# Second layer in pieces of 512, 512, 384, 384 and 384 columns, and a lag of three steps with loads two steps ahead in the first layer

## The chip, the cores and the metric

The kernel runs on one core of one Trainium2 chip. The metric is device microseconds of one execution. TensorE is PE in the rows (PEld its weight loads), VectorE is DVE, ScalarE is ACT, and SyncE is SP, whose queue issues nearly all DMAs.

## The reference, cut to what matters

```python
x, state: (8 batches, 8 heads, 512 | 32, 64)
a     = softmax(scale * x @ state.T);   xread = a @ state
a2    = softmax(scale * state @ x.T);   sread = a2 @ x
x = concat([xread, sread])              # 8 * (512 + 32) = 4352 tokens of 512
h = x @ w_in;  r = max(h, 0);  x = (s * r * r + b) @ w_out      # first layer, 512 -> 2048 -> 512
h = x @ w_in;  g = h / (1 + exp(-h));  out = g @ w_out          # second layer, same sizes
```

All is asked for in float32. The weights arrive as 64-bit floats.

## The kernel before, in words

**Precision.** Each factor of a product is split into a high and a low part (line 218 `copy` on ACT rounds to the high part, line 221 `rest` on DVE subtracts), and each product is three matmuls: high by high, high by low, low by high (lines 533 and 866).

**First layer.** Tokens are worked off in nine blocks (line 102): the 512 `x` tokens of each batch, blocks 0 to 7, and at last the 256 `state` tokens of all batches, block "s". Block 0 is interleaved by a list written out by hand (lines 36 to 77, `first`, line 1151) with the weight conversion and the attention of batches 0 and 1. The others go through `run` (line 627): a block has 16 steps, one for each 128 rows of the hidden layer. One step of a 512-wide block:

- `mm1_a` (line 538): six matmuls into a bank `ph` (pool of two banks);
- `act_a` (line 570): relu on ACT (572), `s*r*r` on DVE (573). The second half, `gh = r + b` on ACT (578) and `gl = r + b - gh` on DVE (579), is put off by `late` and issued by `finish` (line 559) at the beginning of the next step;
- `flush(LAG)` (line 655): `mm2_a` (line 597), twelve matmuls of 512 columns, for the step LAG = 2 before. When that was the last step of a block, `end_a` (line 611) follows: four banks are copied out (lines 606 and 608) and four DMAs write them to `x2` (line 618);
- the step's extras, `do(f, 0)` ahead of `mm1_a` and `do(f, 2)` at the end (line 1377 `extra`): the attention of the next batch, loads and splits of `G` (lines 308 and 318), and what `convert` (line 1262) has set down.

`r`, `gh` and `gl` have three buffers each (line 564).

**Conversion of the second layer's weights** runs beside blocks 1 to 7. `convert` gives each pair of weights six steps: `load64` (line 152, two DMAs of 512 KB into one of two `raw` buffers) ahead of step `at`, where `at` is 16 + 3u with u even; `absw` (line 176, ACT) at the end of step `at + 1`; then the bit operations (`bits`, line 180, DVE, four for each half of the pair), `reorder`, `keep` (a DMA to `kept`) and `sum_w` (four DVE operations and two DMAs). Block 2 begins with step 32, block 5 with step 80, so a pair's `load64` falls on step f = 2 of each of those two blocks.

In the rows ACT, DVE and SP each work through their instructions in program order.

**Block "s" and the places.** `last_block` (line 1286) hands tiles that are free by then to a queue `spare`; everything in the second layer takes its tiles from its front and gives them back at its end (`Place`, line 684). `v24` to `v31` are handed over at the first step, `wh` and `wl` of step f - 2 at step f (line 1304).

**Second layer.** Seven products in the place of eight (`PRODUCTS`, line 82, with sums of inputs and of weights). The tokens are cut into two halves of 2176, and each half into five pieces (lines 673 to 675): four of 448 columns and one of 384. `first_product` (line 967) goes through all pieces: for each, eight `Quad`s of seven steps with six matmuls each (line 867), 336 matmuls a piece. ACT copies and applies silu, DVE adds and subtracts, and the results go to DRAM (`go`, line 903), one DMA a step on the average. While a piece runs, the next one's inputs are loaded and split: 14 `high`s on ACT and 14 `low`s on DVE, one of each in a step, from step 46 of the piece's 56 (lines 1356 to 1358). The last A22 product of a Quad is put into step 2 of the next one (line 973).

Then `Chunks` (line 1080) does the second product in the same pieces: 56 chunks a piece, each with one load from `go` (line 1096), one high, one low and six matmuls, 336 a piece again. Loads run twelve chunks ahead. Every third step `load_o` (line 1446) loads output weights until all are there. Twelve chunk loads and the first twelve output weights are issued in the last piece of the first product (lines 1359 to 1367). Transposed results go out by `put` (line 1049).

Of the kernel before, what the change touches and what calls it, by code (L numbers as in the profile page):

```python
# [13 lines left out]
F32R = mybir.dt.float32r  # L14
# [10 lines left out]
NF = DFF // P  # L25
# [1 line left out]
NT = B * SB  # L27
SCALE = 0.125
EPS = 1e-9
LAG = 2  # L30
NU = 16
RING = 8

# [54 lines left out]
def fused_kernel(ctx: ExitStack, tc, xt, xn, sbd, sg, w1, w2, sv, bv, out):  # L88
# [32 lines left out]
    def space(tag, shape=(P, S), dtype=F32R):  # L121
        return wpool.tile(list(shape), dtype, tag=tag, name=tag)
# [3 lines left out]
    def rot(name, n, shape=(P, S), dtype=F32):  # L126

        i = turns[name] = turns.get(name, -1) + 1
        return space(f"{name}{i % n}", shape, dtype)
# [429 lines left out]
    def finish():  # L559

        while late:
            late.pop(0)()

    def new_act(n):
        r = rot("r", 3)
        gh = rot("gh", 3, dtype=F32R)
        gl = rot("gl", 3, dtype=F32R)
        return r[:, :n], gh[:, :n], gl[:, :n]

    def act_a(ph, n, bi):  # L570
        r, gh, gl = new_act(n)
        nc.scalar.activation(out=r, in_=ph[:, :n], func=AF.Relu)  # L572
        nc.vector.scalar_tensor_tensor(  # L573
            out=r, in0=r, scalar=s_sb, in1=r, op0=ALU.mult, op1=ALU.mult
        )

        def second():
            nc.scalar.activation(out=gh, in_=r, func=AF.Identity, bias=b_sb)  # L578
            nc.vector.scalar_tensor_tensor(  # L579
                out=gl, in0=r, scalar=b_sb, in1=gh.bitcast(F32), op0=ALU.add, op1=ALU.subtract  # L580
            )

        late.append(second)
        return gh, gl
# [12 lines left out]
    def mm2_a(f, g, n):  # L597
        gh, gl = g
        w = "o", f
        cs = [slice(c * P, (c + 1) * P) for c in range(NC)]  # L600
        mm2(f, [(wh[w][:, c], wl[w][:, c], gh[:, :n], gl[:, :n]) for c in cs], n)
# [9 lines left out]
    def end_a(k):  # L611
        n = width[k]
        for c in range(NC):
            o = pull_out(c, n)
            o = o[:, :n]
            if k == "s":
                o = o.rearrange("p (b r) -> p b r", r=NS)
            nc.sync.dma_start(out=rows(c, k), in_=o)
# [8 lines left out]
    def run(blocks, pend):  # L627


        def flush(upto):  # L630
            while len(pend) > upto:
                i, f, g = pend.pop(0)
                k = blocks[i]
                mm2_a(f, g, width[k])
                if f == NF - 1:
                    end_a(k)

        for i, k in enumerate(blocks):
            if i == 0:
                continue  # L640
            ops = extra(i)

            def do(f, when):
                for op in ops.get((f, when), ()):
                    op()

            for f in range(NF):
                do(f, 0)
                finish()
                pend.append((i, f, act_a(mm1_a(f, k), width[k], i)))  # L650
                do(f, 1)
                last = f == NF - 1 and i + 1 == len(blocks)
                if last:
                    finish()
                flush(LAG)
                if f == NF - 1 and not last:
                    prepare_a(blocks[i + 1])
                if last:
                    flush(0)
                do(f, 2)  # L660
# [10 lines left out]


    HALF = NT // 2
    WIDE = 448
    pieces = [(at, min(WIDE, HALF - at)) for at in range(0, HALF, WIDE)]
    sums = {(t, i, n): dram.tile([P, S], F32, name=f"sums_{t}{i}_{n}")
            for t in "IO" for i in range(NF // 2) for n in range(2)}
    go = {(k, p): dram.tile([NF // 2, P, n], F32, name=f"go_{k}_{p}")
# [3 lines left out]
    spare, fixed, closing = deque(), deque(), []  # L682
# [37 lines left out]
    def sub_(out, a, b):  # L720
        tt(out, a, b, ALU.subtract)
# [83 lines left out]
    class Inputs:  # L805
# [19 lines left out]
        def sum(self, name, c):  # L825
            to, a, b = {
                "T1": ("T1", "B12", "B11"), "T2": ("T2", "B22", "T1"),
                "T3": ("B12", "B22", "B12"), "T4": ("B21", "B21", "T2"),
            }[name]
            if (to, c) not in self.x:  # L830
                self.x[to, c] = Place(F32)
            to, a, b = (self.x[x, c] for x in (to, a, b))
            sub_(to.t[:, :self.n], a.t[:, :self.n], b.t[:, :self.n])
            self.x[name, c] = to
# [316 lines left out]
    def first():  # L1151

        halves = {n + str(b): Half(b, j) for b in range(2) for j, n in enumerate("pq")}
        act = {}
# [100 lines left out]

        for name in FIRST.split():
            one(name.rstrip("*"), name.endswith("*"))
        return [(0, f, act[f][1:]) for f in range(NF - LAG, NF)]

    later, quads = {}, {}  # L1260

    def convert():

        def add(at, when, op, *args):
            later.setdefault((at, when), []).append(lambda: op(*args))

        for u in range(2 * NF):
            i, t = u // 4, "IO"[u // 2 % 2]  # L1270
            pair = (t, i), (t, i + NF // 2)
            at = NF + 3 * u
            if u % 2 == 0:
                add(at, 0, load64, pair)
                add(at + 1, 2, absw, pair)
            for op, n in enumerate((2, 2, 3, 3)):
                add(at + n, 2, bits, pair, op, u % 2)
            if t == "O":
                add(at + 4, 2, reorder, pair, u % 2)
            add(at + 5, 2, keep, pair[u % 2])  # L1280
            if u % 2:
                x = sum_w(t, i)
                for n in range(5, 8):
                    add(at + n, 2, next, x)

    def last_block(add):

        def give(*tags):  # L1290
            add(f, 2, spare.extend, tags)

        splits = [(p, c) for p in RIGHT for c in range(2)]
        inputs[0] = Inputs(0)
        for f in range(NF):
            if f == 0:
                give("xt0", "xt1", "xn0", "xn1", *(f"mid{i}" for i in range(4)), "sbd",
                     "xh2", "xh3", "xl2", "xl3", *(f"v{i}" for i in range(24, 32)),
                     *(f"xr{i}" for i in range(4)))
                for i in range(2):  # L1300
                    add(f, 2, carve, f"raw{i}", 4)
                add(f, 2, inputs[0].load)
            if f >= 2:
                give(f"wh{f - 2}", f"wl{f - 2}")
            if f == 7:
                give(*(f"v{i}" for i in range(8, 16)))
            if f == 11:
                give(*(f"v{i}" for i in range(8)))
            if f == 15:
                give(*(f"v{i}" for i in range(16, 24)))  # L1310
            if 2 <= f < 4:
                for name in ("T1", "T2", "T3"):
                    add(f, 2, inputs[0].sum, name, f - 2)
            for i, what in ((f - 4, inputs[0].high), (f - 5, inputs[0].low)):
                if 0 <= i < len(splits) // 2:
                    for p, c in splits[2 * i:2 * i + 2]:
                        add(f, 2, what, p, c)
            for i, what in ((f - 6, "load"), (f - 9, "high"), (f - 10, "low")):
                if i >= 0 and i % 2 == 0 and i // 2 < 5:
                    if what == "load":  # L1320
                        quads[i // 2] = list(duos_in(i // 2))
                    for x in quads[i // 2]:
                        add(f, 2, getattr(x, what))
# [103 lines left out]
    with tc.manual_schedule():  # L1427

        warm = small.tile([P, 1], F32, tag="nm", name="warm")
        nc.gpsimd.memset(warm, 0.0)  # L1430
        nc.scalar.activation(out=warm, in_=warm, func=AF.Exp)
        make_identity(nc, ident)
        pend = first()
        convert()
        run(order, pend)
        spare.extend(f"{n}{i}" for n in ("wh", "wl") for i in (NF - 2, NF - 1))
        spare.extend(f"{n}{i}" for n in ("r", "o", "gh", "gl") for i in range(3))
        spare.extend(f"{n}{i}" for n in ("xh", "xl") for i in range(2))
        for tag in ("wf0", "wf1", "xs"):
            carve(tag, 2)  # L1440
        chunks = Chunks()
        to_load = iter([
            Duo(("O", i, p), ("O", i + 1, p)) for p in RIGHT for i in range(0, NF // 2, 2)
        ])

        def load_o(k=0, n=0):
            if k == 0 and n % 3 == 0:
                for x in islice(to_load, 1):
                    x.load()
                    after(6, x.high)  # L1450
                    after(7, x.low)

        steps = hooks(chunks, load_o)
        first_product(steps, lambda: chunks.step(load_o))
        while chunks.step(load_o):
            tick()
        while due:
            tick()
# [44 lines left out]
```

## Time and profile before

| what | us |
|---|---|
| median of 3 runs | 1374.11 |
| the runs | 1370.12, 1374.11, 1382.07 |
| the profiled execution | 1378.16 |
| its span in the trace | 1376.3 |
| PE busy in it | 1350.4 |

The rows below are from the profiled execution and count from the beginning of its span. A matmul's own duration in them is longer than the distance to the next one's start, since matmuls are pipelined; the distance of the starts is what a matmul costs. In rows of a timeline, idle time before the instruction stands in brackets with what ended it.

### The profile page before, as it was taken

Reading aid. Unit: us, or ns where it says so; the run is one execution under the profiler, and the core shown is the slowest. Engines: PE = TensorE matmul, PEld = TensorE weight load, DVE = VectorE, ACT = ScalarE, POOL = GpSimd, SP = SyncE. Lnnn points to the kernel's source line nnn. Section 1 sums busy time; section 2 is a strip of 40 time slices with the busy share of each in tenths; the row PEclk is TensorE's granted clock in tenths of the full one; section 3 lists DMA queues with packets and bytes.
Section 4 is the critical chain, followed back from the end, with each engine's and each line's share of the span. In section 5 each row is a group of like instructions: output and inputs, shape, how many; then the busy total and the mean of one; then the engine's idle time right before and its main releaser. Section 6 shows DMA issues by size and latency. Waiting matters only on the chain.

```text
span 1376.3 us, 19962 instructions
## 1 busy us (share of the span) xinstructions
PE 1350.4 (98%) x6648; PEld 1189.0 (86%) x6648; DVE 988.4 (72%) x1770; ACT 750.0 (54%) x1389; POOL 0.7 (0%) x7
## 2 busy tenths in 40 slices
PE   6999999999999999999999999999999999999998
PEld 4778888788888788888999999999998999999997
DVE  7899877788788778755877757575767756464655
ACT  7999644455545455444665646464656735353542
POOL 0000000000000000000000000000000000000000
PEclk9999999999999999999999999999999999999999
DMA  9999335454434535322648565656679895959593
GB/s 324 331 332 317 132 116 167 130 186 145 160 127 130 185 102 170 121 100 62 227 151 283 186 238 184 238 184 230 216 256 327 301 280 151 280 152 281 142 272 88
DMA packets 180999, 275.55 MB, mean 200 GB/s; under 512 B 22688, under 2 KB 133280, under 8 KB 180896
## 3 DMA queue, kind: packets, MB, share of 16 engines
q1 hardware_dynamic: 180096, 273.88, 60.6%
q8 instruction: 52, 0.85, 0.3%
q10 hardware_dynamic: 800, 0.39, 0.1%
q14 instruction: 51, 0.42, 0.1%
HBM read 158.34 MB, written 115.87 MB: 199 GB/s over the span
## 4 chain that ended last, share of the span: by engine, by line
PE 88%; DMA 4%; DVE 3%; ACT 2%; issue 1%; SPq 1%; DVEq 0%; ACTq 0%
PE bank L867 48%; PE o L593 24%; PE ph L534 12%; DMA raw<-w 3%; PE bank L509 2%; PE bank L270 2%; PE bank L534 1%; ACT xr L218 1%; DVE v L221 0%; PE bank L465 0%; DVE wf L195 0%; DMA go<-v 0%; ACT wf L178 0%; DMA xt<-xt 0%; DMA wl<-sums_O 0%
## 5 line engine op out<-in xcount | busy, mean ns | idle before, releaser
L593 PE MATMUL o<-gl,wh 128*128 128x512 f32 (+1 forms) x576 | 218.4, 379 | 3.7 <-DVE gl L579 3.6
L593 PE MATMUL o<-gh,wh 128*128 128x512 f32 (+1 forms) x576 | 218.4, 379 | 0.2 <-ACT gh L578 0.2
L593 PE MATMUL o<-gh,wl 128*128 128x512 f32 (+1 forms) x576 | 218.2, 379 | 0.0
L534 PE MATMUL ph<-xh,v 128*128 128x512 f32 (+1 forms) x640 | 204.9, 371 | 0.0
L572 ACT ACTIVATE r<-ph 128x512 f32<-128x512 f32 (+1 forms) x128 | 72.5, 566 | 145.5 <-PE ph L534 143.1
L573 DVE SCALAR_TENSOR_TENSOR r<-r,s_sb 128x512 f32<-128x512 f32 (+1 forms) x128 | 91.5, 715 | 68.5 <-ACT r L572 68.2
L534 PEld LDWEIGHTS ph<-xh,v 128*128 128x128 f32 x640 | 117.2, 189 | 20.2 <-ACT xr L218 0.5
L593 PEld LDWEIGHTS o<-gl,wh 128*128 128x128 f32 x576 | 108.8, 189 | 25.6 <-DVE gl L579 5.4
L593 PEld LDWEIGHTS o<-gh,wh 128*128 128x128 f32 x576 | 108.8, 189 | 20.6 <-ACT gh L578 0.6
L593 PEld LDWEIGHTS o<-gh,wl 128*128 128x128 f32 x576 | 108.7, 189 | 20.2
L579 DVE SCALAR_TENSOR_TENSOR gl<-r,b_sb,gh 128x512 fp32r<-128x512 f32 (+1 forms) x128 | 91.3, 713 | 42.3 <-ACT gh L578 41.6
L534 PE MATMUL ph<-xl,v 128*128 128x512 f32 (+1 forms) x320 | 117.8, 368 | 0.0
L578 ACT ACTIVATE gh<-r,b_sb 128x512 fp32r<-128x512 f32 (+1 forms) x128 | 88.6, 692 | 53.0 <-DVE r L573 53.0
L867 PE MATMUL bank<-v,v 128*128 128x448 f32 (+1 forms) x292 | 91.7, 360 | 0.0
L534 PEld LDWEIGHTS ph<-xl,v 128*128 128x128 f32 x320 | 60.4, 189 | 9.6
L218 ACT ACTIVATE v<-v 128x512 fp32r<-128x512 f32 (+2 forms) x103 | 60.6, 597 | 11.0 <-PE bank L867 6.9
L715 DVE TENSOR_TENSOR v<-bank,v 128x448 f32<-128x448 f32 (+1 forms) x49 | 29.7, 606 | 47.3 <-PE bank L867 43.9
L867 PEld LDWEIGHTS bank<-v,v 128*128 128x128 f32 x292 | 54.6, 188 | 3.9
L867 PE MATMUL bank<-v,wh 128*128 128x448 f32 (+1 forms) x163 | 54.1, 362 | 0.0
L867 PE MATMUL bank<-v,wl 128*128 128x448 f32 (+1 forms) x163 | 53.5, 361 | 0.0
L218 ACT ACTIVATE v<-bank 128x448 f32<-128x448 f32 (+1 forms) x42 | 22.3, 530 | 55.0 <-PE bank L867 54.5
L221 DVE TENSOR_TENSOR v<-v,v 128x512 fp32r<-128x512 f32 (+2 forms) x77 | 50.6, 665 | 1.5 <-ACT v L218 1.4
(1006 smaller groups left out, 3119.0 us busy)
## 6 DMA issues: line engine op xcount, KB each, us to landing
raw<-w SPq DMA_DIRECT2D x64, 512.0 KB, 6.0
v<-go SPq DMA_DIRECT2D x84, 224.0 KB, 4.3
go<-v SPq DMA_DIRECT2D x58, 224.0 KB, 2.3
gd<-xr SPq DMA_DIRECT2D x48, 256.0 KB, 4.0
go<-wl SPq DMA_DIRECT2D x44, 224.0 KB, 2.2
wl<-go SPq DMA_DIRECT2D x42, 224.0 KB, 4.5
v<-gd SPq DMA_DIRECT2D x32, 256.0 KB, 4.3
wh<-go SPq DMA_DIRECT2D x35, 224.0 KB, 4.2
```

Source lines behind the costliest of these rows:

```text
L218: nc.scalar.activation(out=out, in_=x, func=AF.Copy)
L221: nc.vector.tensor_tensor(out=lo, in0=x, in1=hi.bitcast(F32), op=ALU.subtract)
L270: nc.tensor.matmul(t, a[p][:, cs], x[w], start=i == 0, stop=i == 2)
L509: nc.tensor.matmul(o[:, k, :], xn_t[self.b, self.j, t // 2][:, t % 2, k * P:(k + 1) * P], self.a2[:, t * P + 2 * k * NS:t * P + 2 * (k + 1 ...
L534: nc.tensor.matmul(ph[:, :n], a, x, start=j == 0 and i == 0, stop=j == last and i == 2)
L572: nc.scalar.activation(out=r, in_=ph[:, :n], func=AF.Relu)
L573: nc.vector.scalar_tensor_tensor(out=r, in0=r, scalar=s_sb, in1=r, op0=ALU.mult, op1=ALU.mult)
L578: nc.scalar.activation(out=gh, in_=r, func=AF.Identity, bias=b_sb)
L579: nc.vector.scalar_tensor_tensor(out=gl, in0=r, scalar=b_sb, in1=gh.bitcast(F32), op0=ALU.add, op1=ALU.subtract)
L593: nc.tensor.matmul(po[c][:, :n], a, x, start=f == 0 and i == 0, stop=f == NF - 1 and i == 2)
L715: nc.vector.tensor_tensor(out=out, in0=a, in1=b, op=op)
L867: nc.tensor.matmul(bank[:, :n], a, x, start=start and j == 0 and i == 0, stop=stop and j == last and i == 2, skip_group_check=True,)
```

## The change

The second layer's pieces become 512, 512, 384, 384 and 384 columns (the sum is 2176 as before). In the first layer the lag goes from two steps to three; `gh` and `gl` get a fourth pair of buffers, `v30` and `v31`, from block 1 on, so that these two join `spare` only after `run`. In `convert`, all but the load of a pair comes one step later.

```diff
-LAG = 2
+LAG = 3
...
+    act_places = deque((f"gh{i}", f"gl{i}") for i in range(3))
+
     def new_act(n):
         r = rot("r", 3)
-        gh = rot("gh", 3, dtype=F32R)
-        gl = rot("gl", 3, dtype=F32R)
+        gh, gl = (space(tag) for tag in act_places[0])
+        act_places.rotate(-1)
         return r[:, :n], gh[:, :n], gl[:, :n]
...
-    WIDE = 448
-    pieces = [(at, min(WIDE, HALF - at)) for at in range(0, HALF, WIDE)]
+    widths = 512, 512, 384, 384, 384
+    pieces = [(sum(widths[:k]), n) for k, n in enumerate(widths)]
...
-        return [(0, f, act[f][1:]) for f in range(NF - LAG, NF)]
+        return [(0, f, act[f][1:]) for f in range(NF - 2, NF)]
...
-            at = NF + 3 * u
+            at = NF + 1 + 3 * u
             if u % 2 == 0:
-                add(at, 0, load64, pair)
+                add(at - 1, 0, load64, pair)
                 add(at + 1, 2, absw, pair)
...
-                     "xh2", "xh3", "xl2", "xl3", *(f"v{i}" for i in range(24, 32)),
+                     "xh2", "xh3", "xl2", "xl3", *(f"v{i}" for i in range(24, 30)),
...
         convert()
+        act_places.appendleft(("v30", "v31"))
         run(order, pend)
         spare.extend(f"{n}{i}" for n in ("wh", "wl") for i in (NF - 2, NF - 1))
         spare.extend(f"{n}{i}" for n in ("r", "o", "gh", "gl") for i in range(3))
+        spare.extend(("v30", "v31"))
```

## Rows read from the trace of the kernel before

**Rows 1.** The page, busy time of the engines (share of the span).
```profile
PE 1350.4 (98%) x6648; PEld 1189.0 (86%) x6648; DVE 988.4 (72%) x1770; ACT 750.0 (54%) x1389; POOL 0.7 (0%) x7
```

**Rows 2.** Waits of PE: us in total, times, longest.
```profile
PE o L593 <- DVE gl L579: 3.6, 3, 2.1
...
PE bank L867 <- DVE gl L221: 0.6, 1, 0.6
PE bank L867 <- DVE o L221: 0.4, 1, 0.4
```

**Rows 3.** Timeline of PE in the second layer: start, duration, instruction.
```profile
700.68 0.57 PE L867 MATMUL bank<-raw,wh 128*128 128x448 f32 x2
...
977.14 0.34 PE L867 MATMUL bank<-wl,wh 128*128 128x384 f32 x1
...
1035.59 0.37 PE L867 MATMUL bank<-xr,xn 128*128 128x448 f32 x1
...
1311.07 0.34 PE L867 MATMUL bank<-v,xn 128*128 128x384 f32 x1
...
1344.70 0.33 PE L867 MATMUL bank<-v,wl 128*128 128x384 f32 x1
...
1354.58 0.33 PE L867 MATMUL bank<-wl,wh 128*128 128x384 f32 x1
```

**Rows 4.** Chain that ended last, first layer: start, duration, what.
```profile
175.54 1.73 PE bank L509 x16
...
253.52 1.73 PE bank L509 x16
...
302.56 2.72 PE o L593 x12
...
398.81 1.73 PE bank L509 x16
...
472.98 1.73 PE bank L509 x16
...
545.64 1.73 PE bank L509 x16
```

**Rows 5.** Timeline of SP, beginning of block 2.
```profile
222.80 1.48 SPq L618 DMA_DIRECT2D x<-o  x3
...
226.22 1.28 SPq L157 DMA_DIRECT2D raw<-w  x2
```

**Rows 6.** Timeline of ACT, blocks 2 and 5.
```profile
235.20 1.12 ACT L178 ACTIVATE wf<-raw 128x1024 f32<-128x1024 f32 x1 [2.91 <-DMA raw<-w]
...
456.25 1.12 ACT L178 ACTIVATE wf<-raw 128x1024 f32<-128x1024 f32 x1 [0.70 <-DMA raw<-w]
```

**Rows 7.** Timeline of PE, block 2.
```profile
249.14 0.54 PE L593 MATMUL o<-gl,wh 128*128 128x512 f32 x1 [2.09 <-DVE gl L579]
...
250.33 0.63 PE L593 MATMUL o<-gl,wh 128*128 128x512 f32 x1
```

**Rows 8.** Windows: us, length, busy by engine (PE, PEld, DVE, ACT, POOL), granted clock, DMA share, GB/s.
```profile
250.00:252.00 2.00, 2.00 (x6) 1.56 (x5) 2.00 (x4) 1.50 (x3) 0.00 (x0) 0.50 0.02 7
...
460.00:464.00 4.00, 4.00 (x21) 3.30 (x20) 3.93 (x9) 1.28 (x3) 0.00 (x0) 1.00 0.00 0
...
1040.00:1060.00 20.00, 19.44 (x97) 17.67 (x96) 14.09 (x26) 11.98 (x24) 0.00 (x0) 1.00 0.99 336
```

**Rows 9.** Timeline of DVE, splits of the fourth piece's inputs, and 384-wide operations later.
```profile
898.58 0.62 DVE L221 TENSOR_TENSOR v<-xh,wl 128x448 fp32r<-128x448 f32 x1
...
908.88 0.62 DVE L715 TENSOR_TENSOR wh<-bank,wh 128x448 f32<-128x448 f32 x1
...
914.77 0.62 DVE L221 TENSOR_TENSOR wh<-r,xt 128x448 fp32r<-128x448 f32 x1
...
1039.64 0.55 DVE L715 TENSOR_TENSOR wl<-v,wl 128x384 f32<-128x384 f32 x1
1040.11 0.55 DVE L715 TENSOR_TENSOR v<-v,wh 128x384 f32<-128x384 f32 x1
```

## The prediction

> **What bounds the kernel now.** First the page: PE is busy 1350.4 of 1376.3 us [rows 1], so all idle time of PE together is 25.9 us, and a gain beyond some of that must come from matmuls that get cheaper. Then the waits of PE: 3.6 us behind `gl` in the first layer, 0.6 and 0.4 us in the second [rows 2]; the rest of the idle time lies at the two ends of the span, which the diff does not touch. A busy share does not say what one matmul costs, so next the timeline of PE, and in it the distances of the starts. In the first layer twelve matmuls of 512 columns take 2.72 us [rows 4], 226.7 ns each. In the second layer, 384-wide ones take (1354.58 - 1344.70) / 57 = 173.3 ns [rows 3] (57 matmuls lie between these two starts). At 2.4 GHz that is 544 and 416 cycles, columns plus 32 in both. The 448-wide ones should then take 200.0 ns. They don't: four pieces of 336, less the six that slip behind the next piece, take 977.14 - 700.68 = 276.46 us, which is 206.6 ns each, and PE waits for nothing there. In the second product, 1035.59 to 1311.07 holds 1344 of them, six of 384 (1.04 us) and the waits of 1.0 us [rows 2, 3]: 273.4 us, 203.5 ns each. So 448 columns are dear in this kernel, by 6.6 and 3.5 ns; why, no row says.
>
> Last the chain, which runs through PE nearly everywhere, and in it a mark that returns once in each block [rows 4]: 253.52 to 398.81 is two blocks, 72.65 us each; 472.98 to 545.64 is 72.66. But 175.54 to 253.52 takes 77.98 us, 5.33 too many, and 398.81 to 472.98 takes 74.17, 1.52 too many. Those are blocks 2 and 5. There ACT stood 2.91 and 0.70 us before `absw`, until the `raw` DMA had landed [rows 6]. SP had issued it at 226.22, behind the four writes of `end_a` from 222.80 on [rows 5]. Everything behind `absw` on ACT came late, relu and `gh` with it; DVE was full afterwards (3.93 of 4 us in 460 to 464) [rows 8] and `gl` came 2.09 us late for PE [rows 7]. After that wait the granted clock fell to 0.50, the 1.2 GHz level, in 250 to 252 [rows 8], where six matmuls stand in 2 us [rows 7, 8] in place of nine. So 6.85 us of the profiled execution are lost in two places of the first layer.
>
> **The widths.** The number of matmuls is the same (336 a piece in each product), the last piece is still 384 wide, and only the first four change. First product: 672 at 226.7 ns and 666 at 173.3 are 152.3 + 115.4 = 267.8 us in place of 276.5: 8.7 us gained. Second: 672 x (0.2267 + 0.1733) = 268.8 us, with 1.0 of 384s and 1.0 of waits 270.8 in place of 275.5: 4.7 us. Together 13.4 us. The unknown is the rate of 512 columns on line 867, where no row has that width: 226.7 ns by the first layer's rows at least; at most with the surcharge of the 448s on top, 233.3 and 230.2 ns, which takes 672 x (0.0066 + 0.0035) = 6.8 us back. I take the first, because 384 has no surcharge on that very line.
>
> The Trainium skill (TensorE: Matmul & The Clock Gate, "Back-to-back issue gap") gives the gap of a matmul as N / 2.4 + 2.5 ns, a straight line in the columns. By it five pieces with the same sum cost the same, and the term would be nothing; the trace has 384 and 512 on one line with another constant (13.3 ns) and 448 off it.
>
> What the widths cost: DVE and ACT operations come in the same number, and their time too goes with the sum of columns. The tight place is where a piece's 14 splits stand beside the Quads. From 898.58 to 914.77 DVE starts 29 operations, about 0.535 us apart when it doesn't wait, 15.5 of 16.7 us [rows 9]. 384-wide ones start 0.47 us apart [rows 9], so 29 take 13.6 us; the 13.5 steps of that stretch shrink from 1.24 to 1.04 us, 14.0 us. DVE goes from 93% to 97%, still below PE. The nearest due time: the add on the bank at 908.88 ends at 909.50, and the A22 matmuls that want this bank start twelve matmuls after the piece's start, 977.14 - 336 x 0.2066 + 2.48 = 910.20; 0.7 us to spare, which with shorter steps becomes about 0.3. I put 0.5 us for the two transitions between 384-wide pieces (bounds 0 and 2). Where the two products meet, DMA is at 0.99 [rows 8] and the two waits of 1.0 us are; twelve chunk loads become 32 KB larger, 0.39 MB or 1.2 us at 336 GB/s, but the steps behind become 1.36 us long in place of 1.22. I put 0.5 us more (bounds -1.0 and +1.2).
>
> **Lag and loads.** `load64` stays at its step, and `absw` and all behind it come one step (4.08 us) later. With a lag of three, `end_a` moves from step f = 1 to f = 2 and so behind the `load64` of f = 2: SP issues that load ahead of the four writes, about 3.4 us earlier [rows 5]. Against a wait of 2.91 us that is 7.5 us; the wait on `raw` goes, with 4.6 us to spare. And `gl` of a step is wanted one step later, so that DVE may fall behind by 4.08 us more; in block 5 a lateness of 1.52 us came almost without a wait for `raw`. Expected: all blocks at 72.65 us, 6.85 us less. What it adds: the four writes and the `keep` now queue on SP behind `load64`; the buffer `r` that one of them reads is wanted three steps later, 12 us, and the `raw` DMA had landed 235.20 - 226.22 = 9.0 us after its issue [rows 5, 6]. Bit operations meet the attention's operations on DVE one step later; the sets come every three steps and a block has 16, so each alignment of the two has occurred already, and four of the seven blocks with one are clean. A buffer of `gh` is written one step behind its last `mm2`, as before (four buffers, lag three). In block "s" `spare` has two tiles fewer; by counting takes and gives, at least eight stay. `wh` of step f - 2 is handed over before its last `mm2` is issued, but taken a step later at the earliest; a copy may then wait for twelve 256-wide matmuls, 1.44 us, which the longer lag covers (2.88 us). The first block's list is as before, and its last two `mm2` move one step back. I put nothing for all this (bounds 0 and 3).
>
> **The sum.** 8.7 + 4.7 + 6.85 - 0.5 - 0.5 = 19.25 us off the profiled execution's 1378.16: 1358.9. That execution is 4.05 us above the median of the runs. If the difference lies elsewhere than in blocks 2 and 5, the new median is 1354.9; if it is all there, only 2.8 us are left to gain in the first layer, 1374.11 - 13.4 - 2.8 + 1.0 = 1358.9. I take the middle, 1357.0, that is 1.2% faster. Measurement tells about 1%, 13.7 us, from no change: the widths alone just miss that.
>
> **Rivals.**
> - *The stalls of the first layer were not in the median run, or come back elsewhere.* For it: the fastest run, 1370.12, lies 8.0 us below the profiled one, nearly the 6.85. Against it: the order on SP makes the wait likely each time. 1374.11 - 13.4 + 1.0 = 1361.7.
> - *The surcharge belongs to line 867, not to 448 columns.* For it: it differs between the two products, 6.6 and 3.5 ns, so operands matter. Against: 384 pays none on the same line. 1357.0 + 6.8 = 1363.8.
> - *The widths are worth nothing*, 512 on this line being so dear that the sum is the same (some 237 ns). For it only that a cost linear in columns would give as much; against it the rows. 1357.0 + 13.4 = 1370.4. That is what the page's rule would make of it.
> - *Slower: DVE falls behind PE in the split stretch.* The place is the 14 splits before each of the four later pieces of the first product; PE then waits for an add before A22, and the clock falls as it did in block 2. The price of such a wait with its slow stretch is 5.33 us [rows 4]; four are 21.3: 1378.3. It decides where DVE has more than 1.04 / 0.47 = 2.2 operations a step; 29 in 13.5 steps are 2.15. Near, but the 512-wide pieces have 1.36 us a step, and most parts are wanted several steps after they are made.
>
> **How the numbers follow.** Forecast 0.74 (its own range 1352 to 1361), no gain in the first layer 0.08, surcharge at 512 0.07, widths worth nothing 0.02, DVE behind 0.05, and 0.04 for something else at the transition of the products, 2 to 5 us. The range 1351 to 1366 leaves out the fourth and fifth and the tails. Faster by over 1% means below 1360.4: most of the forecast and some of the next two, 0.72. Slower by over 1% would take more than the priced rival: 0.03. Within 1%: 0.25.
>
> **What would show it.** On line 867 starts 226.7 ns apart at 512 and 173.3 at 384; the second layer from its first matmul to its last in some 654 to 657 us; the mark of the blocks 72.65 us apart everywhere, no wait of ACT for `raw` after the first block, the clock at 1.00 around 250. I am wrong if 512 columns cost over 230 ns there, if a block still takes over 74 us, or if PE waits for DVE or a bank where pieces change.

## The result, and the profile after

Four runs of the kernel after: 1356.46 to 1360.73 us, median 1358.24; four of the kernel before beside them: median 1372.53. The ratio is 0.9891, with a 95% interval of 0.9867 to 0.9916: 1.1% faster, against 1.2% forecast (1357.0 us).

The profiled execution took 1358.0 us, its span is 1356.2 us, 20.1 less than before. Line numbers have moved by three (867 is now 870, 593 is 596, 579 is 582). First the page's busy time and, from the waits of PE, the only one that is left after the first block (from 140 us on):

```profile
PE 1333.1 (98%) x6648; PEld 1167.2 (86%) x6648; DVE 988.4 (73%) x1770; ACT 751.2 (55%) x1389; POOL 0.7 (0%) x7
```
```profile
PE bank L870 <- DVE gl L221: 0.3, 1, 0.3
```

PE does the same 6648 matmuls in 17.3 us less, while DVE and ACT are as busy as before to 1.2 us [rows 1]. The waits for `gl` of the first layer are gone [rows 2]. Then the same mark of the blocks as before [rows 4], from the chain that ended last:

```profile
172.97 1.73 PE bank L509 x16
...
245.60 1.73 PE bank L509 x16
...
318.23 1.73 PE bank L509 x16
...
390.87 1.73 PE bank L509 x16
...
463.50 1.73 PE bank L509 x16
...
536.13 1.73 PE bank L509 x16
```

All distances are 72.63 or 72.64 us; blocks 2 and 5 no longer take 77.98 and 74.17. SP and ACT show that block 2 no longer waits for `raw`. The timelines of the two, to be held against [rows 5] and [rows 6]:

```profile
219.68 1.25 SPq L157 DMA_DIRECT2D raw<-w  x2
223.33 1.71 SPq L621 DMA_DIRECT2D x<-o  x3
```
```profile
233.72 1.13 ACT L178 ACTIVATE wf<-raw 128x1024 f32<-128x1024 f32 x1
```

The load of `raw` now goes out ahead of the four writes, and `absw` starts at 233.72 with no idle time before it. Last the second layer, in the timeline of PE, where [rows 3] have the answering starts:

```profile
693.68 0.63 PE L870 MATMUL bank<-raw,sbd 128*128 128x512 f32 x2
...
844.67 0.33 PE L870 MATMUL bank<-wh,sbd 128*128 128x384 f32 x1
...
1019.77 0.40 PE L870 MATMUL bank<-xr,v 128*128 128x512 f32 x1
...
1174.44 0.33 PE L870 MATMUL bank<-wl,v 128*128 128x384 f32 x1
```

844.67 - 693.68 is 150.99 us for 666 matmuls of 512 columns, 226.7 ns each: no surcharge on this line. The first matmul of the second layer starts at 693.68 (before: 700.68), so the first layer gave 7.0 us between these two profiles; to the end of the span it is 662.5 us from there (before: 675.6), so the second layer gave 13.1.

### The profile page after: what moved, and what is told of

Read it like the earlier page. It is cut to its first block, busy times and chain, and to the rows that moved or that the text cites. A ratio compares the mean times of both kernels' runs of the same rounds, so it can differ in the third digit from the quotient of the medians.

```text
span 1356.2 us, 19968 instructions
## 1 busy us (share of the span) xinstructions
PE 1333.1 (98%) x6648; PEld 1167.2 (86%) x6648; DVE 988.4 (73%) x1770; ACT 751.2 (55%) x1389; POOL 0.7 (0%) x7
## 4 chain that ended last, share of the span: by engine, by line
PE 91%; DMA 3%; ACT 3%; DVE 1%; issue 1%; SPq 0%; ACTq 0%; DVEq 0%
PE bank L870 47%; PE o L596 26%; PE ph L534 14%; PE bank L509 2%; PE bank L534 1%; PE bank L270 1%; DMA gd<-xr 1%; ACT xr L218 1%; DMA kept_i<-wf 1%; DMA raw<-w 0%; DMA v<-sg 0%; PE bank L465 0%; DMA go<-v 0%; DMA go<-xl 0%; ACT wf L178 0%
## 5 line engine op out<-in xcount | busy, mean ns | idle before, releaser
L596 PE MATMUL o<-gh,wh 128*128 128x512 f32 (+1 forms) x448 | 169.5, 378 | 0.0
L596 PE MATMUL o<-gh,wl 128*128 128x512 f32 (+1 forms) x448 | 169.3, 378 | 0.0
L596 PE MATMUL o<-gl,wh 128*128 128x512 f32 (+1 forms) x448 | 169.2, 378 | 0.0
L870 PE MATMUL bank<-v,v 128*128 128x384 f32 (+1 forms) x276 | 83.1, 357 | 0.0
L596 PE MATMUL o<-v,wh 128*128 128x512 f32 (+1 forms) x256 | 74.9, 376 | 0.0
L870 PE MATMUL bank<-v,wl 128*128 128x384 f32 (+1 forms) x199 | 64.7, 357 | 0.0
L870 PE MATMUL bank<-v,wh 128*128 128x384 f32 (+1 forms) x201 | 63.4, 351 | 0.0
L218 ACT ACTIVATE v<-v 128x512 fp32r<-128x512 f32 (+1 forms) x100 | 58.2, 593 | 8.7 <-PE bank L870 6.5
L718 DVE TENSOR_TENSOR v<-bank,v 128x384 f32<-128x384 f32 (+1 forms) x51 | 30.9, 606 | 36.0 <-PE bank L870 29.8
L596 PEld LDWEIGHTS o<-v,wh 128*128 128x128 f32 x256 | 47.0, 188 | 8.7
```

The source lines that it names most:

```text
L218: nc.scalar.activation(out=out, in_=x, func=AF.Copy)
L596: nc.tensor.matmul(po[c][:, :n], a, x, start=f == 0 and i == 0, stop=f == NF - 1 and i == 2)
L718: nc.vector.tensor_tensor(out=out, in0=a, in1=b, op=op)
L870: nc.tensor.matmul(bank[:, :n], a, x, start=start and j == 0 and i == 0, stop=stop and j == last and i == 2, skip_group_check=True,)
```

## The experiments

**Each part alone, and the kernel before once more.** Three kernels of one set of runs; beside them 13 runs of the kernel before, 1371.11 to 1380.93 us, median 1374.34.

The widths alone, with the first layer as before:

```diff
-    WIDE = 448
-    pieces = [(at, min(WIDE, HALF - at)) for at in range(0, HALF, WIDE)]
+    widths = 512, 512, 384, 384, 384
+    pieces = [(sum(widths[:k]), n) for k, n in enumerate(widths)]
```

> The new widths with the old lag and the old loads. Theory: 13 us less than before in every execution (ratio 0.9905), the second layer 655 us long, and the blocks of the first layer as before, block 2 over 72.65 us. Rival (the widths need the shifted first layer, by the places that they take from the spare queue): less than 10 us.

Measured: 1362.47 to 1366.28, median 1364.38 us; ratio 0.9921 (0.9893 to 0.9950), some 10 us. The second layer is as in the kernel after. In the first, the marks show the old loss:

```profile
176.20 1.73 PE bank L509 x16
...
251.98 1.73 PE bank L509 x16
...
397.27 1.73 PE bank L509 x16
...
470.98 1.73 PE bank L509 x16
```

Block 2 takes 75.78 and block 5 takes 73.71 us, 3.1 and 1.1 too many. So the widths are worth some 10 us without the other part. The interval, 7 to 15 us, holds the 13 expected of "every execution" and the rival's less than 10, so these times don't decide between the two. Block 2 lost 5.3 us in the profile of before. PE waited as long for `gl` here (2.07 us, until 249.19), but the clock stayed at 1.00, where [rows 8] have 0.50:

```profile
250.00:252.00 2.00, 2.00 (x12) 1.67 (x10) 2.00 (x4) 1.56 (x3) 0.00 (x0) 1.00 0.01 2
```

The first layer's part alone, with the old widths:

```diff
-    widths = 512, 512, 384, 384, 384
-    pieces = [(sum(widths[:k]), n) for k, n in enumerate(widths)]
+    WIDE = 448
+    pieces = [(at, min(WIDE, HALF - at)) for at in range(0, HALF, WIDE)]
```

> The new lag, buffers and loads with the old widths of 448. Theory: all blocks of the first layer at 72.65 us and no wait of ACT for raw after the first block; the second layer stays at 668 us. As the median of the runs before fell to 1372.5, some 14 us above the kernel after, 1 to 3 us less than before (ratio 0.998 to 0.999). Rival (the profiled 6.85 us are lost in each execution): 5 to 7 us less, ratio 0.995 to 0.996.

Measured: median 1367.15 us of ten runs, ratio 0.9948 (0.9927 to 0.9969), some 7 us. All blocks at 72.63 or 72.64 us. The rival with 5 to 7 us was right, and what I had drawn from the small sample of medians was wrong. The second layer was not 668 us long either: from 693.09 to the end of the span it was 670.1, 5.5 less than in the first profile of before; the next experiment has 670.8. The two parts alone make 17 us together, the kernel after had 14.3 in its own runs; each interval is 3 to 4 us to either side, so that is no contradiction and no proof that they add up.

The kernel before, a second profile:

> The kernel before once more, for a second profile of it. Theory (the lateness in blocks 2 and 5 comes from the order on SP and is there in every execution, but its size follows how fast the raw DMA lands): the mark of the blocks returns after 72.65 us in blocks 3, 4 and 6 and after more than that in block 2 or block 5, by 0.5 to 6 us in sum. Rival (the profiled execution was a rare one): all blocks at 72.65 us. In both, the 448-wide matmuls of the second layer start 206.6 ns apart in the first product and about 203 in the second, and the second layer takes 668 us from its first matmul to its last.

Measured: 1371.84 us. The marks stand at 175.12, 324.56 (two blocks, 149.44), 397.19 and 471.53 (74.34), so 4.2 and 1.7 us are lost around blocks 2 and 5, 5.9 together. With 6.9 and 4.2 in the two other profiles that have the old first layer, the loss is in each of three executions. How large it is does not follow from the wait for `raw` alone. The timeline of ACT, two rows of the first profile of before (blocks 3 and 6, which take 72.65 and 72.66 us) and one of the widths alone (block 5, 1.1 us too many):

```profile
291.41 1.12 ACT L178 ACTIVATE wf<-raw 128x1024 f32<-128x1024 f32 x1 [1.24 <-DMA raw<-w]
...
511.50 1.12 ACT L178 ACTIVATE wf<-raw 128x1024 f32<-128x1024 f32 x1 [1.86 <-DMA raw<-w]
```
```profile
454.25 1.12 ACT L178 ACTIVATE wf<-raw 128x1024 f32<-128x1024 f32 x1 [0.20 <-DMA raw<-w]
```

Waits of 1.24 and 1.86 us cost PE nothing there, and behind one of 0.20 PE waited 0.8 us. What makes block 5 late besides `raw` is not shown. In the second layer the first four pieces took 970.42 - 699.24 = 271.18 us, not 276.46: 202.7 ns for one 448-wide matmul, not 206.6. The expectation failed there.

**Which of the two edits of the first layer does it.** Widths of 448 in both; beside them 13 runs of before, 1369.33 to 1384.98, median 1379.35.

The lag alone, with the conversion at its old steps (on top of the first layer's part):

```diff
-            at = NF + 1 + 3 * u
+            at = NF + 3 * u
             if u % 2 == 0:
-                add(at - 1, 0, load64, pair)
+                add(at, 0, load64, pair)
```

> Widths of 448, the lag of three with its buffers, but the conversion at its old steps. Theory (the order on SP is what matters: end_a now comes behind load64, so raw lands some 3.4 us earlier; and gl is due a step later): all blocks at 72.65 us, no wait of PE in blocks 1 to 7, ACT's wait for raw under 1 us in sum; ratio to before 0.995 as with both. Rival (the loads two steps ahead do it): block 2 stays over 74 us. The 448-wide matmuls: 202.7 ns on the mean of three in most phases, 206.6 in some.

Measured: ratio 0.9930 (0.9906 to 0.9953). All blocks at 72.6 us, and no wait of PE from 140 to 690 us. ACT still waits for `raw`, more than the 1 us that I gave it, but in blocks 3 and 6 (until 283.79, 478.20 and 501.75), not in 2 and 5, and PE waits for nothing behind it; in the waits of ACT, 140 to 650 us (us in total, times, longest):

```profile
ACT wf L178 <- DMA raw<-w: 3.5, 3, 1.4
```

A lag of three changes two things, the order on SP and the time at which `gl` is due; no run has one of them without the other.

The loads alone, with a lag of two and three buffers:

```diff
-LAG = 3
+LAG = 2
...
-        act_places.appendleft(("v30", "v31"))
```

> Widths of 448, the lag of two with three buffers, and the conversion one step later behind its load. Theory: ACT's wait for raw goes (4.08 us more against 2.9 at most), but gl is still due after two steps while DVE is full, so that 0.5 to 2 us stay lost in some blocks; ratio 0.996. Rival (raw was the only cause): all blocks at 72.65 us, as with the lag alone.

Measured: ratio 0.9964 (0.9935 to 0.9993), and no wait of PE from 140 to 690 us. The marks:

```profile
174.74 1.73 PE bank L509 x16
...
247.37 1.73 PE bank L509 x16
...
392.64 1.73 PE bank L509 x16
...
465.27 1.73 PE bank L509 x16
```

Block 2 takes 72.63 us, and block 5 too. The rival was right in what it forecast: with `absw` and the bit operations behind it a step later, the lag of two is enough. Here `raw` goes out behind the four writes still (at 224.94) and ACT does not wait for it in those blocks. So either edit alone took the loss of these two blocks away, in one profile each, and the two together add nothing that the profiles or the ratios show (lag 0.9930, loads 0.9964, both 0.9948 beside other runs of before; the intervals overlap). That `raw` was the only cause is not shown by it, since the bit operations on DVE moved too.

**What one matmul costs at each width.** Five widths in one kernel:

```diff
-    widths = 512, 512, 384, 384, 384
+    widths = 512, 480, 448, 416, 320
```

> Pieces of 512, 480, 448, 416 and 320 columns, the rest as in the kernel after: what one matmul costs at each width. Theory (only multiples of 128 columns lie on the line of columns plus 32 cycles): starts 226.7 ns apart at 512, and surcharges of about 6 ns on 213.3 at 480, 200.0 at 448, 186.7 at 416 and 146.7 at 320. Rival A (448 alone, or widths near it, are dear): 320 and 416 without a surcharge. Rival B (multiples of 64 are enough and 448 suffers for another reason): 320 without, 416 and 480 with a surcharge.

The timeline of PE, the first start of each width (448 and 416 in the first product, then 480, 448, 416 and 320 in the second):

```profile
841.65 0.36 PE L870 MATMUL bank<-wh,sbd 128*128 128x448 f32 x1
...
911.09 0.35 PE L870 MATMUL bank<-wh,sbd 128*128 128x416 f32 x1
...
1105.55 0.38 PE L870 MATMUL bank<-v,v 128*128 128x480 f32 x1
...
1178.35 0.36 PE L870 MATMUL bank<-wl,v 128*128 128x448 f32 x1
...
1246.44 0.54 PE L870 MATMUL bank<-v,v 128*128 128x416 f32 x2
...
1309.72 0.30 PE L870 MATMUL bank<-v,v 128*128 128x320 f32 x1
```

In the second product the distances divided by 336 are 216.7, 202.7 and 188.3 ns for 480, 448 and 416 columns. In the first product 448 cost (69.44 - 1.30) / 330 = 206.5 (six late 480s taken off), in the same execution. 320-wide ones start 146.7 ns apart. That is what rival B forecast: 320 has no surcharge, and 416 and 480 have one, of 1.7 and 3.3 ns, beside the 2.7 or 6.6 of 448. The theory fails at 320, and rival A at 416.

Two narrower widths:

```diff
-    widths = 512, 512, 384, 384, 384
+    widths = 512, 512, 512, 352, 288
```

> Pieces of 512, 512, 512, 352 and 288 columns: which narrower widths pay a surcharge. Theory (only widths between 384 and 512 do, since 320 does not): 160.0 ns at 352 and 133.3 at 288. Rival (what is not a multiple of 64 does): some 2 ns more at both.

Measured: 161.1 ns at 352 (336 of them from 1255.10 to 1309.23) and 131.7 at 288. So 352 pays 1.1 ns, and 288 is 1.6 ns below the line. The theory failed at both widths, the rival at 288. All together, in ns from start to start, with (columns + 32) / 2.4 GHz beside it:

| columns | line | measured | widths of the pieces with it |
|---|---|---|---|
| 256 | 120.0 | 120.0 | 512, 512, 512, 384, 256 |
| 288 | 133.3 | 131.7 | 512, 512, 512, 352, 288 |
| 320 | 146.7 | 146.7 | 512, 480, 448, 416, 320 |
| 352 | 160.0 | 161.1 | 512, 512, 512, 352, 288 |
| 384 | 173.3 | 173.4 | most |
| 416 | 186.7 | 188.3 | 512, 480, 448, 416, 320 |
| 448 | 200.0 | 202.7 or 206.6 | 448 four times and 384; five widths |
| 480 | 213.3 | 216.7 | 512, 480, 448, 416, 320 |
| 512 | 226.7 | 226.7 | most |

The four widths that are not multiples of 64 are all off the line; of the five multiples of 64 only 448 is. That is a pattern of nine widths, not a cause.

**Is it where the operands stand?** Two kernels with 448-wide pieces, the outputs in the last 448 columns of their banks, or the moving operands in the last 448 columns of their tiles:

```diff
-                self.x = bank("h", [P, S])
+                self.x = bank("h", [P, S])[:, S - self.n:]
...
```

> Both parts of the first layer's change, widths of 448, and every product of the second layer written to the last 448 columns of its bank, not the first. It tells where the surcharge of 448 columns sits. If it depends on where in the bank the output stands, the distances differ from 199, 203 and 207 ns in turn (mean 202.7, or 206.6 throughout); at 200.0 throughout the cause would be found. If it comes from the number of columns alone or from the operands read: the same distances as before.

```diff
-                self.of.mm(p, i, [y.t[:, :self.of.n] for y in two])
+                self.of.mm(p, i, [y.t[:, S - self.of.n:] for y in two])
...
```

> As the last, but with the outputs at the bank's beginning and the moving operands (high and low parts) in the last 448 columns of their tiles. If the surcharge depends on where the moving operand begins in SBUF, the distances change, to 200.0 or to 206.6 throughout; if it comes from the number of columns alone, they stay at 199, 203 and 207 in turn or 206.6 throughout.

With the outputs moved, 202.7 ns in the first product and 206.7 in the second; with the operands moved, 202.7 in both. The two values are the same as ever, so the surcharge did not go when either place was moved by 64 columns. Eight profiles have 448-wide pieces, that is 16 products: 11 have 202.7 and 5 have 206.6 ns, sometimes the first product (the profile of before, the five widths, the loads alone), sometimes the second (the lag alone, outputs moved). From its first 70 matmuls or so a product keeps its value to the end. At 202.7 the distances are 199, 203 and 207 ns, mixed; at 206.6 nearly all are 206 or 207. For a product of 1344 such matmuls the difference is 5.3 us. The lag alone shows both in one execution; starts of its first 448s and the first 384s behind them, in either product:

```profile
693.92 0.57 PE L870 MATMUL bank<-raw,sbd 128*128 128x448 f32 x2
...
965.09 0.33 PE L870 MATMUL bank<-r,sbd 128*128 128x384 f32 x1
...
1027.89 0.36 PE L870 MATMUL bank<-wh,wh 128*128 128x448 f32 x1
...
1304.87 0.34 PE L870 MATMUL bank<-v,v 128*128 128x384 f32 x1
```

271.17 us for 1338 of them, 202.7 ns each; in the second product 276.98 for the last 1332, with two waits of PE that cost 1.9 us among them, 206.5 each. Near its beginning the value changes twice, each time at such a wait:

```profile
1031.82 0.47 PE L870 MATMUL bank<-gl,v 128*128 128x448 f32 x1 [1.09 <-DVE gl L221]
...
1042.10 0.47 PE L870 MATMUL bank<-wl,wf 128*128 128x448 f32 x1 [0.28 <-DVE wl L221]
```

The twelve 448-wide matmuls before the first wait start 206 or 207 ns apart, the 48 between the two 202.7 on the mean, and those behind the second 206.6. A wait is not needed, though: the dear first products (in the profile of before, the five widths and the loads alone) have their first twelve 448-wide matmuls at some 203 and are dear from there, with no wait of PE between.

**A version that might beat it, and the kernel after again.** Eleven runs of before beside them: 1368.95 to 1379.44, median 1372.81.

```diff
-    widths = 512, 512, 384, 384, 384
+    widths = 512, 512, 512, 384, 256
```

> The kernel after with pieces of 512, 512, 512, 384 and 256 columns: all on the line of columns plus 32 cycles, the same number of matmuls. Theory: 512 and 256 at 226.7 and 120.0 ns, so PE's time is the same; the end after the last matmul becomes some 1 us shorter, as the last output write is 512 KB and not 768; the transition between the products becomes dearer, as twelve chunk loads of 256 KB meet steps of 0.72 us, by 1 to 5 us: 0 to 4 us slower than the kernel after (ratio to before 0.989 to 0.992). Rival (the loads run far enough ahead): 1 us faster than the kernel after.

Measured: median 1364.09 us, ratio 0.9932 (0.9911 to 0.9954), some 6 us slower than the kernel after; more than the 4 that I allowed. The waits of PE in its profile:

```profile
PE bank L870 <- ACT v L218: 2.5, 1, 2.5
...
PE bank L870 <- ACT wl L218: 0.9, 1, 0.9
PE bank L870 <- ACT wh L218: 0.8, 1, 0.8
...
PE bank L870 <- DVE v L221: 0.5, 1, 0.5
...
PE bank L870 <- DVE gh L221: 0.3, 1, 0.3
```

All of them lie where the two products meet. 512 and 256 columns are on the line, so the matmuls cost the same at full clock; the transition costs 5.0 us of waits where the kernel after has 0.3 and, in its second profile below, 1.0. The granted clock was 0.83 from 1030 to 1040 us, behind the wait of 2.5 us.

> The kernel after once more, beside the last one, for a second profile and more runs. Theory: without 448-wide pieces no phase can be of the dear kind, and no block late, so its runs scatter less than those of before: within 5 us of each other, against 10 to 15 us; median 1356 to 1360. Rival (the scatter comes from the start, where loads bind): as wide as before's.

Measured: four runs, 1356.59 to 1360.06, median 1358.34; ratio 0.9893 (0.9869 to 0.9918). With the four runs above, eight lie within 4.3 us; each set of before spreads over 10 to 16 us. The theory held. The widths alone, with the late blocks, lie within 3.8 us too (four runs), while the lag and loads with widths of 448 spread over 8.7 (ten runs): the scatter goes with the widths, as far as sets of unequal size tell. That the two kinds of 448-wide products make a good part of before's spread fits (0, 5.3 or 10.6 us), but only profiled executions show the kind, so it is not shown for the others.

## Why the prediction was right, and where by luck

- **The widths.** The steps were right: 512 columns at 226.7 ns on this line, 13.4 us by the profile's rows, 13.1 between the two profiles (8.8 in the first product, 4.3 in the second). But a term was mis-sized for the typical run: I read 206.6 and 203.5 ns as two products with a surcharge each of its own. They were the two values of one width, and the profile of before had the dear one in the first product. At 202.7 in both, four pieces cost 2 x 1344 x 2.7 ns = 7.3 us too many, and each dear product 5.3 more; with 5 dear of 16, some 10.6 us on the mean. The widths alone measured 10, with an interval that holds 13 as well; the profiles are sharper. From its first matmul to the end of the span the second layer takes 670.1 to 671.4 us in the three with four pieces of 448 and no dear product, 675.7 to 676.2 in the four with one, and 662.2 to 663.6 in the three with the new widths. What I called 3.5 ns in the second product was 2.7 and small delays where the products meet.
- **The median and the profiled execution.** I split their 4.05 us between "elsewhere" and blocks 2 and 5. The loss in those blocks was there in all three profiles of the old first layer, 4.2 to 6.9 us; the dear product alone is 5.3. So the 13.4 was too much for the typical run, and the first layer's share (2.8 at the lower end) too little. The errors went opposite ways: 10 and 7 us, each part alone, where the sum behind the forecast had 13.4 and 2.8 to 6.85. That they nearly cancelled, and left the median 1.2 us above the forecast, is luck.
- **Lag and loads.** The wait of PE for `gl` that the forecast named is gone, at 7.0 us between the two profiles in place of 6.85. Over all profiles it is less: the second layer begins at 698.93 to 700.68 in the three with the old first layer and at 692.96 to 695.48 in the ten with a changed one, 5.7 us earlier on the mean. The step that the runs correct is the margin of 7.5 us as one thing: with either half, 3.4 from SP's order or 4.08 from the later `absw`, ACT has no wait for `raw` in blocks 2 and 5. Whether that wait made all of the lateness in block 5 stays open. Six matmuls "in place of nine" in 250 to 252 was misread: the count of a window takes in those begun before it, and the same stretch at clock 1.00 has 12. No wait of PE came from what I priced at nothing.
- **DVE where pieces change.** I put 0.5 us; the profile after has no such wait. DVE got as full as forecast, 97%: 13.59 of 14.00 us with 29 operations, where the first 384-wide piece gives way to the second:

```profile
895.22:909.22 14.00, 14.00 (x83) 14.00 (x82) 13.59 (x29) 11.46 (x27) 0.00 (x0) 1.00 0.51 180
```

- **The transition of the products.** I put 0.5 us more; the waits are 0.3 us in place of 1.0 [rows 2], but 1.0 again in the second profile of the kernel after, so no gain and no loss is shown. The 256-wide last piece shows what it costs when the steps ahead of the transition get short.
- **The rivals.** A surcharge of line 867 as such is out (512 and 384 pay none there in the kernel after), and so is a first layer without gain. That the widths are worth nothing is out too: 512 columns would have to cost some 237 ns and cost 226.7. The Trainium skill (TensorE: Matmul & The Clock Gate, "Back-to-back issue gap") has N / 2.4 + 2.5 ns, by which the widths would be worth nothing, but for an isolated matmul, which the prediction left out; for a stream of weight loads and matmuls it has some 131 ns at N = 512. The trace, which is of such a stream, agrees with neither: 226.7 ns at 512, another constant (13.3 ns) and widths off any straight line.

## What to carry to other kernels

Read what a matmul costs from the distance of the starts, for each width by itself: a busy share of 98% hid 7 to 13 us here, and widths with the same sum and the same number of matmuls differ by that much, up to a per cent of the kernel. Before a gain is taken from one profile, look at a second one: a term that differs between executions (here 202.7 or 206.6 ns) is otherwise sold as what the change is worth. And where two edits remove the same wait, one of them may do.

## What the runs showed that I had not expected

Of the nine widths tried, 256, 320, 384 and 512 columns cost columns plus 32 cycles at 2.4 GHz; 352, 416, 448 and 480 cost 1.1 to 6.6 ns more, 288 costs 1.6 ns less. 448 has two values. A product keeps one from its first 70 matmuls or so to its end, and moving the outputs or the moving operands by 64 columns left both as they were. In the one product of 16 that changed twice, the changes stand at waits of PE. Why these widths, and what chooses between the two values, is open: nothing here was tried on the weight loads, which stand between all these matmuls.
